# A first stage's instruction list made anew: maxima subtracted on VectorE for four sub-blocks, low parts of x formed in PSUM for five

## The chip, the cores and the metric

The kernel runs on one core of a Trainium2 chip. The metric is the device time of one execution in microseconds, as a median over runs; the traces show one execution each. TensorE is called PE in the views, VectorE DVE, ScalarE ACT, GpSimd POOL and SyncE SP. PE's weight loads stand apart as PEld.

## What is computed

```python
def _attn_ref(q, k, v):                      # batch 8, heads 8, seq 576, head_dim 64
    scores = scale * np.matmul(q_c, k_c.transpose(0, 1, 2, 4, 3))   # chunks of 64 tokens
    scores = scores - np.max(scores, axis=-1, keepdims=True)
    attn = np.exp(scores)
    attn = attn / (np.sum(attn, axis=-1, keepdims=True) + 1e-09)
    return np.matmul(attn, v_c)

def _moe_ref(x, w_in, w_out, alpha):         # x: 4608 tokens x 512, d_ff 2048
    h = x @ w_in
    g = np.maximum(h, 0.0) + alpha * np.minimum(h, 0.0)
    return g @ w_out
```

q, k and v are float32, the weights arrive as float64 patterns. The output of the attention, with the heads side by side, is x.

## The kernel before

The 4608 tokens make 36 sub-blocks of 128 tokens (two chunks of 64 each), and nine blocks of 512 tokens. The d_ff axis is cut into 16 slices f of 128. Every product of the two layers is made in three passes out of high and low parts (high x high, high x low, low x high), each of the matmuls 128x128 by 128x512. `h` of a block and a slice is 12 such matmuls into one bank of `ps_h` (line 422); its share of the output, called `o` here, is 12 more into `ps_oa` and `ps_ob` (line 458). Between the two, ACT forms the negative part (line 407), DVE the PReLU (410), ACT the high part `gh` (436) and DVE the low part `gl` (439). `ps_h` has two buffers, so an `h` can start only when line 410 of the `h` two before it has read its bank.

Blocks 0 and 1 (eight sub-blocks, the **first stage**) need their attention before anything else can run. Each sub-block s goes through scores `S` (line 261), maxima `m` (298), exponentials `z`/`e` (304 or 313), sums and normalisation `a`, `r`, `n` (317 to 323), four transposes `T` through PSUM (349), their copy `p` (356), values `V` (367), and the two parts of x: `x` (high, ACT, line 373) and `l` (low, DVE, line 375). The exponentials have two forms. A sub-block in `SUBTRACTED` has its maxima subtracted by DVE, one exponential over 128x512 on ACT, and its sums formed by DVE. The others have the maximum as ACT's bias, and so take eight exponentials of 128x64, each with its sum.

While that runs, weights are fetched (`wi3`, `wo3`: a DMA of 512 KB on SP's queue) and split: `wi3b`, `k`, `h`, `u`, `v`, `i`, `j` are the seven steps of `piece`, two on ACT and five on DVE (`wi0` has all on DVE).

All of this is an order written out by hand, the string `START`: each token makes its instructions, and every engine runs its own in the order of the list. `W8` are eight filler matmuls of 128x128 on zeros. `q`, `k`, `v` load two sub-blocks at a time. `h02 R02 G02 gh02 gl02 o02` are the steps of block 0, slice 2. `K0` to `K3` store the partial sums of block 0. `BANKS` names the PSUM banks that S, T and V of a sub-block use, `HALVES` the work buffer of a weight. The list ends with block 1, slice 7. After it a scheduler with a cost model of its own orders the instructions of the remaining steps; there the weights are fetched and split by `prepare`, and `keep_a` (line 597, POOL's queue) stores quarters of the split weights, from the moment at which POOL's `table` copy has seen the last part of x of block 1. Later stages, from block 2 on, are untouched.

Of the kernel before, what the change touches and what calls it, by code (L numbers as in the profile page):

```python
# [19 lines left out]
def bits(pattern):  # L20
# [5 lines left out]


START = """
W8 q0 k0 k1 q1 q2 S0 W1 k2 m0 S1 W5 wi1 z0 m1 e0 wi0 z1 a0 e1 r0 S2 k4 n0 S3 m2 q4 wi1b z2 T0 W6 m3
e2 a1 z3 wi1k v0 wi0b r1 wi1h n1 wi2 p0 wi0k T1 a2 e3 wi0h r2 S4 W3 v2 wi0u n2 m4 q6 p1 V0 a3 z4  # L30
wi0v e4 T2 W4 k6 r3 wi0i wi1u wi0j wo4 wi1v x0 V1 n3 p2 wo0 l0 x1 V2 wi2b a4 l1 T3 x2 wo1 wi2k S5 p3
l2 wi1i V3 m5 v6 S6 r4 x3 z5 n4 e5 wi4 l3 h00 m6 v4 wi2h z6 wi1j e6 wi2u S7 wi3 a5 wi2v h01 m7 wo2
r5 R00 z7 n5 wo0b G00 wi5 wi2i T5 e7 wo0k wi2j h02 wi7 a6 wo0h r6 wo0u wo5 n6 p5 wo0v gh00 T6 wo1b
a7 T4 wo3 gl00 wo0i V5 r7 wo1k p6 wo0j x5 V6 n7 p4 l5 x6 T7 wo1h V4 l6 p7 wo1u x4 o00 R01 wo1v wo2b
G01 wo1i l4 gh01 wo1j R02 V7 gl01 o01 x7 wo2k G02 wi4b wi3b wo2h wo2u gh02 l7 h10 wo2v gl02 wo2i
wi3k wo2j wi4k wo4b o02 wi3h wi4h R10 wo4k wi4u K0 wi3u K1 G10 h11 wi4v gh10 wi3v wi4i gl10 K2 wi3i
wo4h wi4j K3 o10 wo4u wo5b wi3j R11 wo4v wi5b G11 wo4i wo6 h12 wo5k gh11 wo4j wi6 gl11 wo3b wo5h
wo3k wo5u wo8 o11 R12 wo3h wo5v wi8 G12 wo5i wo3u gh12 wo7 h13 wo5j gl12 wi7b wo3v wi5k wo3i wi7k
wi5h o12 R13 wo3j wi5u G13 wi5v gh13 h14 wi7h wi5i gl13 wi6b wi5j wi6k wi7u wi6h o13 R14 wi7v G14
wi7i wi6u gh14 wo6b wi6v h15 gl14 wi6i wo6k wi6j wi7j wo7b wo6h o14 wo7k R15 wo6u G15 wo6v gh15 wo7h  # L40
wi8b gl15 h16 wo6i wo7u wo7v wo6j wo7i wi8k o15 wo7j R16 wo8b G16 wi8h gh16 wi8u gl16 h17 wi8v wo8k
wi8i wi8j wo8h o16 R17 G17 wo8u gh17 wo8v gl17 wo8i wo8j
"""
# [12 lines left out]
LISTED = 18

# [2 lines left out]
def tile_local_attention_prelu_ffn(  # L60
# [63 lines left out]
    def place(name, shape, dtype):  # L124
        return sides[name[:2]][0].tile(shape, dtype, name=name)
# [15 lines left out]
    FREE = 12  # L141
    RAWS = 6
# [89 lines left out]
    def attn_load(s, parts="qkv"):  # L232
# [61 lines left out]
    def early_softmax(s, sc3):  # L294
# [412 lines left out]
    banks = ["ps_h", "ps_h", "ps_o0", "ps_o1", "ps_o2", "ps_o3"]  # L707
# [171 lines left out]
    def start(token):  # L879

        name, at = re.fullmatch(r"([a-zA-Z]+)(\d+)([a-z]?)", token).group(1, 2)
        s = int(at)
        if name in ("wi", "wo"):
            if token[-1].isdigit():
                fetch(name, s)
            elif token[-1] == "b":
                running[name, s] = piece(name, s, f"{name}{s}" in ALONE)
                next(running[name, s])
            else:
                next(running[name, s])  # L890
# [190 lines left out]
```

## Time and profile before

| | us |
|---|---|
| median of 3 runs | 771.2 |
| lowest, highest | 770.76, 772.01 |
| span of the profiled execution | 770.2 |
| busy in the span: PE, DVE, ACT, POOL | 760.4, 646.7, 447.3, 184.8 |

The profiled execution is timed from its first to its last instruction; the median lies 1.0 us above its span, and no time of its own is listed beside the runs. PE's matmuls are pipelined and their ends are modelled, so start-to-start distances say more than durations; the last of a row's instructions reaches past the start of the next row. In a timeline a row is: start, duration, engine, line, operation, out<-in, shape, count, and in brackets the idle time of the engine before it and what ended it.

### The profile page before, as it was taken

Reading aid. Unit: us, or ns where it says so; the run is one execution under the profiler, and the core shown is the slowest. Engines: PE = TensorE matmul, PEld = TensorE weight load, DVE = VectorE, ACT = ScalarE, POOL = GpSimd, SP = SyncE. Lnnn points to the kernel's source line nnn. Section 1 sums busy time; section 2 is a strip of 40 time slices with the busy share of each in tenths; the row PEclk is TensorE's granted clock in tenths of the full one; section 3 lists DMA queues with packets and bytes.
Section 4 is the critical chain, followed back from the end, with each engine's and each line's share of the span. In section 5 each row is a group of like instructions: output and inputs, shape, how many; then the busy total and the mean of one; then the engine's idle time right before and its main releaser. Section 6 shows DMA issues by size and latency. Waiting matters only on the chain.

```text
span 770.2 us, 15415 instructions
## 1 busy us (share of the span) xinstructions
PE 760.4 (99%) x5558; PEld 639.8 (83%) x5558; DVE 646.7 (84%) x1140; ACT 447.3 (58%) x1221; POOL 184.8 (24%) x304
## 2 busy tenths in 40 slices
PE   7999999999999999999999999999999999999998
PEld 7788887888888888888888888888888888888886
DVE  6999988989899886877899898777898977679784
ACT  6975555576666665666657456664574544354643
POOL 1153322343254331111121121111221121122110
PEclk9999999999999999999999999999999999999999
DMA  9859496468798775878765678875656765555573
GB/s 349 337 196 386 176 324 216 163 229 226 234 238 274 240 258 200 304 275 277 263 234 197 233 250 288 269 239 206 207 193 223 260 228 193 204 205 192 198 258 144
DMA packets 69322, 184.52 MB, mean 240 GB/s; under 512 B 10992, under 2 KB 18176, under 8 KB 69120
## 3 DMA queue, kind: packets, MB, share of 16 engines
q0 software_dynamic: 34336, 119.56, 45.9%
q1 hardware_dynamic: 34480, 63.20, 24.2%
q8 instruction: 44, 0.72, 0.4%
q10 hardware_dynamic: 432, 0.79, 0.3%
q14 instruction: 30, 0.25, 0.1%
HBM read 135.27 MB, written 42.99 MB: 231 GB/s over the span
## 4 chain that ended last, share of the span: by engine, by line
PE 92%; ACT 4%; DVE 2%; DMA 2%; issue 0%; ACTq 0%; SPq 0%
PE ps_o L722 20%; PE ps_o L850 19%; PE ps_h L422 14%; PE ps_h L722 10%; PE ps_h L850 10%; PE ps_oa L458 8%; PE ps_ob L458 7%; PE ps_a L388 2%; PE ps_a L272 2%; ACT wi L313 1%; ACT wo L313 1%; DMA raw<-w_in 1%; DMA raw<-w_out 1%; PE ps_h L898 1%; ACT wi L207 0%
## 5 line engine op out<-in xcount | busy, mean ns | idle before, releaser
L422 PE MATMUL ps_h<-xh,wi 128*128 128x512 f32 x384 | 101.7, 385 | 0.7 <-DVE g L410 0.5
L422 PEld LDWEIGHTS ps_h<-xh,wi 128*128 128x128 f32 x384 | 70.7, 187 | 13.8 <-DVE g L410 0.9
L722 PE MATMUL ps_o<-wi,raw 128*128 128x512 f32 x336 | 79.1, 382 | 0.0
L722 PEld LDWEIGHTS ps_o<-wi,raw 128*128 128x128 f32 x336 | 62.5, 187 | 11.2
L678 ACT CAST gh<-wo 128x512 fp32r<-128x512 f32 x66 | 41.0, 620 | 47.4 <-PE ps_o L850 31.8
L287 ACT ACTIVATE pr<-ps_a,mx 128x64 f32<-128x64 f32 x224 | 67.2, 325 | 0.8
L458 PE MATMUL ps_oa<-wo,gh 128*128 128x512 f32 x192 | 58.5, 385 | 0.1
L458 PE MATMUL ps_ob<-wo,gh 128*128 128x512 f32 x192 | 57.7, 380 | 0.0
L422 PE MATMUL ps_h<-xl,wi 128*128 128x512 f32 x192 | 50.6, 381 | 0.0
L679 DVE TENSOR_TENSOR gl<-wo,gh 128x512 fp32r<-128x512 f32 x63 | 43.2, 686 | 7.5 <-ACT gh L678 7.1
L287 ACT ACTIVATION_READ_ACCUMULATOR pr<-ps_a,mx 128x1 f32 x224 | 48.6, 217 | 0.0
L659 POOL DMA_DIRECT2D raw<-wi_a x42 | 22.3, 531 | 102.1 <-PE ps_o L722 54.5
L659 POOL DMA_DIRECT2D raw<-wo_a x42 | 22.2, 529 | 90.8 <-PE ps_o L850 51.2
L407 ACT ACTIVATE wo<-gh 128x512 f32<-128x512 f32 x24 | 15.2, 632 | 48.5 <-DVE gh L752 48.5
L678 ACT CAST ta<-wo 128x512 fp32r<-128x512 f32 x42 | 26.1, 621 | 26.4 <-PE ps_o L850 15.2
L422 PEld LDWEIGHTS ps_h<-xl,wi 128*128 128x128 f32 x192 | 35.8, 187 | 6.7 <-DVE xl L375 0.2
L458 PEld LDWEIGHTS ps_ob<-wo,gh 128*128 128x128 f32 x192 | 35.9, 187 | 6.4
L458 PEld LDWEIGHTS ps_oa<-wo,gh 128*128 128x128 f32 x192 | 35.3, 187 | 7.0 <-ACT gh L436 0.5
L722 PE MATMUL ps_o<-wi,wo 128*128 128x512 f32 x168 | 40.4, 383 | 0.0
L722 PE MATMUL ps_o<-wi,wi 128*128 128x512 f32 x168 | 40.4, 383 | 0.0
L722 PE MATMUL ps_h<-wi,raw 128*128 128x512 f32 x168 | 40.4, 382 | 0.0
L407 ACT ACTIVATE g<-ps_h 128x512 f32<-128x512 f32 x48 | 29.5, 614 | 17.5 <-PE ps_h L422 17.5
(296 smaller groups left out, 2036.2 us busy)
## 6 DMA issues: line engine op xcount, KB each, us to landing
raw<-wi_a POOLq DMA_DIRECT2D x42, 512.0 KB, 4.4
raw<-wo_a POOLq DMA_DIRECT2D x42, 512.0 KB, 3.5
wi<-wi_a POOLq DMA_DIRECT2D x21, 512.0 KB, 3.7
wo<-wi_a POOLq DMA_DIRECT2D x21, 512.0 KB, 4.3
wi<-wo_a POOLq DMA_DIRECT2D x21, 512.0 KB, 3.5
wo<-wo_a POOLq DMA_DIRECT2D x21, 512.0 KB, 3.6
k_sb<-kT SPq DMA_DIRECT2D x28, 256.0 KB, 4.7
q_sb<-qT SPq DMA_DIRECT2D x28, 256.0 KB, 4.1
```

Of the source, the lines that this page charges most:

```text
L272: pe(nc.tensor.matmul(att[0][c * C:(c + 1) * C, par, (NP + hp) * C:(NP + hp + 1) * C], lhsT=q_sb[rows, 2 * hp + c], rhs=kb[rows, 2 * hp + ...
L287: last = nc.scalar.activation(pr[:, g], sc3[:, g // NP, g % NP], AF.Exp, bias=mx[:, g], scale=SCALE, accum_out=sm[:, g])
L313: last = nc.scalar.activation(pr[:, g], sc3[:, g % 2, g // 2], AF.Exp, bias=mx[:, g], scale=SCALE, accum_out=sm[:, g])
L388: pe(nc.tensor.matmul(att[0][par * C:(par + 1) * C, c, hp * C:(hp + 1) * C], lhsT=v_sb[rows, h * C:(h + 1) * C], rhs=p[rows, :, par * NP + ...
L407: nc.scalar.activation(g, h, AF.Relu, scale=-1.0)
L422: pe(nc.tensor.matmul(woven(hps), lhsT=wi[f][:, l, k * P:(k + 1) * P], rhs=woven(xx[:, k]), start=(i == 0 and k == 0), stop=(i == 2 and k ...
L458: pe(nc.tensor.matmul(woven(o), lhsT=a[:, ts], rhs=woven(wo[f][:, l]), start=(f == first and i == 0), stop=(f == last and i == 2),))
L659: streamed[0] = nc.gpsimd.dma_start(out=f32(t), in_=units[side][n])
L678: hi = nc.scalar.copy(t_hi, t)
L679: return hi, nc.vector.tensor_tensor(t_lo, t, f32(t_hi), op=ALU.subtract)
L722: pe(nc.tensor.matmul(woven(ps), lhsT=w[:, l, k * P:(k + 1) * P], rhs=woven(xx[:, xl]), start=first and at == 0, stop=at == n - 1, skip_gr ...
L850: pe(nc.tensor.matmul(woven(ps[m]), lhsT=w[:, l, m * P:(m + 1) * P], rhs=woven(xx), start=i in (1, 5, 2) and j == 0 and n == 0, stop=j == ...
```

## The change

The string `START` is replaced by another list, with `BANKS` and `HALVES` to match. Three things in it are done in another way. `SUBTRACTED` grows from sub-block 0 to 0, 2, 5 and 6. For the sub-blocks in `REMAINDERS` (0 to 4) the low part of x is no longer DVE's subtraction: after ACT has copied the high part, a new token `X` multiplies it by a negated identity on PE and accumulates onto the values in PSUM, and `l` is then an ACT copy of what is left. And a transpose takes a single bank, which can be one of `ps_h`, where it took a pair.

```diff
-W8 q0 k0 k1 q1 q2 S0 W1 k2 m0 S1 W5 wi1 z0 m1 e0 wi0 z1 a0 e1 r0 S2 k4 n0 S3 m2 q4 wi1b z2 T0 W6 m3
...
+k0 q0 W16 S0 m0 k1 q1 z0 W1 S1 e0 q2 m1 k2 z1 a0 r0 e1 W6 S2
...
-SUBTRACTED = (0,)
+SUBTRACTED = (0, 2, 5, 6,)
+REMAINDERS = (0, 1, 2, 3, 4,)
...
+    minus = room(FREE + RAWS + 1, [P, P], F32R)
+    nc.scalar.mul(minus, ident, -1.0)
...
+    pairs = {}
+
     def banks_of(token):
-        pool, name = ((ps_a, "ps_a"), (ps_o, "ps_oa"), (ps_o, "ps_ob"))[BANKS[token]]
-        return pool.tile([P, 2, TB], F32, name=name)
+        pair, bank = divmod(BANKS[token], 2)
+        if pair == 3:
+            return ps_h.tile([P, TB], F32, name="ps_h")
+        if pair not in pairs:
+            pool, name = ((ps_a, "ps_a"), (ps_o, "ps_oa"), (ps_o, "ps_ob"))[pair]
+            pairs[pair] = pool.tile([P, 2, TB], F32, name=name)
+        return pairs[pair][:, bank] if token[0] == "T" else pairs[pair]
...
             pe(nc.tensor.matmul(
-                xo[to, c, cols], lhsT=v_sb[rows, h * C:(h + 1) * C], rhs=p[rows, h * C:(h + 1) * C], start=True, stop=True,
+                xo[to, c, cols], lhsT=v_sb[rows, h * C:(h + 1) * C], rhs=p[rows, h * C:(h + 1) * C],
+                start=hp == 0 or s not in REMAINDERS, stop=True, skip_group_check=hp > 0,
             ))
...
-        nc.vector.tensor_tensor(xl, xo, f32(xh), op=ALU.subtract)
+        if s in REMAINDERS:
+            for c in range(2):
+                pe(nc.tensor.matmul(banks[:, c, :NP * C], lhsT=minus, rhs=xh[:, c], start=False, stop=True, skip_group_check=True))
+            yield
+            nc.scalar.copy(xl, xo)
+        else:
+            nc.vector.tensor_tensor(xl, xo, f32(xh), op=ALU.subtract)
```

Lines move down by 10 to 17 with it: 261 becomes 271, 313 becomes 323, 407 becomes 424, 410 becomes 427, 422 becomes 439.

The beginning of PE's list: fillers (into `ps_h`) and the scores of the first sub-blocks. Before:

```order
L898 MATMUL ps_h<-wo_109 128x128 x8
L261 MATMUL ps_oa<-wo_96,wo_98 64x64 x16
L898 MATMUL ps_h<-wo_109 128x128
L261 MATMUL ps_ob<-wo_96,wo_98 64x64 x16
L898 MATMUL ps_h<-wo_109 128x128 x5
```

And now:

```order
L915 MATMUL ps_h<-wo_109 128x128 x16
L271 MATMUL ps_ob<-wo_96,wo_98 64x64 x16
L915 MATMUL ps_h<-wo_109 128x128
L271 MATMUL ps_oa<-wo_96,wo_98 64x64 x16
L915 MATMUL ps_h<-wo_109 128x128 x6
```

Sixteen fillers stand where eight stood, ahead of the scores of sub-block 0.

ACT's list from the exponentials of sub-block 4 (into `wo_100`) to the last part of x that block 0 needs. Before:

```order
L313 ACTIVATE wo_100,sm<-ps_ob,mx 128x64 x8
L373 CAST xh<-ps_oa 128x2x4x64
L356 COPY wi_103<-ps_a 128x512
L373 CAST xh<-ps_ob 128x2x4x64
L194 ACTIVATE tc<-more 128x512
L373 CAST xh<-ps_a 128x2x4x64
L356 COPY wi_103<-ps_oa 128x512
L207 CAST wi_307<-ta 128x512
L373 CAST xh<-ps_oa 128x2x4x64
```

And now:

```order
L323 ACTIVATE wo_100,sm<-ps_a,mx 128x64 x8
L384 CAST xh<-ps_ob 128x2x4x64
L366 COPY wi_103<-ps_h 128x512
L384 CAST xh<-ps_oa 128x2x4x64
L390 CAST xl<-ps_ob 128x2x4x64
L366 COPY wi_103<-ps_h 128x512
L390 CAST xl<-ps_oa 128x2x4x64
L197 ACTIVATE tb<-raw 128x512
L384 CAST xh<-ps_ob 128x2x4x64
L384 CAST xh<-ps_a 128x2x4x64
L314 ACTIVATE wo_100<-wo_100 128x512
L390 CAST xl<-ps_ob 128x2x4x64
```

Four copies of low parts have come into it (the fourth is the next row, `xl<-ps_a`), and the exponential of sub-block 5 is one instruction.

PE's list just after the hand-written part ends, where block 1 meets slice 8 (`wi8`, split as `wi8_1152` before and `wi8_1160` now). Before, slices 7 and 8 of block 1 follow each other in `ps_h_1614` and `ps_h_1649`:

```order
L422 MATMUL ps_h_1614<-xh_122,wi7_1032 128x4x32x4 x4
L422 MATMUL ps_h_1649<-xh_122,wi8_1152 128x4x32x4 x4
L422 MATMUL ps_h_1649<-xl_123,wi8_1152 128x4x32x4 x2
L458 MATMUL ps_oa_1505<-wo6_1104,gh_1595 128x4x32x4 x2
L458 MATMUL ps_ob_1506<-wo6_1104,gh_1595 128x4x32x4 x2
```

Now, with `ps_h_1348` (slice 8 of block 1), `ps_h_1405` (slice 3 of block 0) and `ps_h_1478` (slice 4 of block 0):

```order
L439 MATMUL ps_h_1348<-xh_126,wi8_1160 128x4x32x4 x4
L439 MATMUL ps_h_1348<-xl_127,wi8_1160 128x4x32x4 x4
L439 MATMUL ps_h_1405<-xh_124,wi3_863 128x4x32x4 x4
L439 MATMUL ps_h_1405<-xl_125,wi3_863 128x4x32x4 x4
L439 MATMUL ps_h_1405<-xh_124,wi3_863 128x4x32x4 x4
...
L475 MATMUL ps_ob_973<-wo7_1133,gl_1231 128x4x32x4
L439 MATMUL ps_h_1348<-xh_126,wi8_1160 128x4x32x4 x4
L439 MATMUL ps_h_1478<-xh_124,wi4_880 128x4x32x4 x4
```

The third pass of slice 8 has moved behind a whole `h` and a whole `o`, directly ahead of the next `h`, which takes the same bank of `ps_h`.

## Rows read from the trace of the kernel before

**Rows 1.** The page's head: the span.

```profile
span 770.2 us, 15415 instructions
```

**Rows 2.** Two stretches: length, busy time of each engine, clock granted, DMA share, GB/s.

```profile
0.00:45.00 45.00, 39.44 (x663) 33.15 (x664) 37.63 (x81) 36.34 (x149) 5.97 (x17) 1.00 0.75 294
45.00:120.00 75.00, 75.00 (x343) 63.74 (x342) 70.59 (x132) 44.21 (x75) 28.64 (x39) 1.00 0.83 296
```

**Rows 3.** Chain of waits of the first 50 us: start, us, what.

```profile
14.48 2.32 ACT wi L313 x16
...
17.05 2.66 ACT wo L313 x16
```

**Rows 4.** Timeline of PE, first stage.

```profile
1.06 3.78 PE L898 MATMUL ps_h<-wo 128*128 128x128 f32 x16 [1.06 <-DVE table L147]
4.77 1.13 PE L261 MATMUL ps_oa<-wo,wo 64*64 64x64 f32 x32
...
6.56 0.97 PE L261 MATMUL ps_ob<-wo,wo 64*64 64x64 f32 x32
...
11.64 1.50 PE L898 MATMUL ps_h<-wo 128*128 128x128 f32 x12
...
15.06 0.69 PE L261 MATMUL ps_ob<-wo,wo 64*64 64x64 f32 x32 [0.34 <-DMA wo<-qT]
...
27.73 1.15 PE L422 MATMUL ps_h<-xh,wi 128*128 128x512 f32 x4
...
30.49 0.60 PE L349 MATMUL ps_ob<-ident,wo 128*128 128x128 f32 x4
...
33.57 0.60 PE L349 MATMUL ps_oa<-ident,wi 128*128 128x128 f32 x4
...
37.80 0.72 PE L458 MATMUL ps_oa<-wo,gh 128*128 128x512 f32 x2
...
44.06 1.04 PE L422 MATMUL ps_h<-xh,wi 128*128 128x512 f32 x4
```

**Rows 5.** Timeline of DVE, first stage.

```profile
5.97 0.69 DVE L298 TENSOR_REDUCE mx<-ps_oa 128x8 f32<-128x512 f32 x1 [4.96 <-PE ps_oa L261]
...
12.70 0.37 DVE L198 TENSOR_SCALAR ta<-ta 128x512 uint32<-128x512 uint32 x1
...
15.23 0.68 DVE L323 TENSOR_TENSOR wi<-wi,sm 128x512 f32<-128x512 f32 x1
15.84 0.68 DVE L298 TENSOR_REDUCE mx<-ps_ob 128x8 f32<-128x512 f32 x1
16.56 0.17 DVE L309 TENSOR_SCALAR mx<-mx 128x8 f32<-128x8 f32 x1
```

**Rows 6.** Timeline of ACT, first stage.

```profile
21.00 0.73 ACT L194 ACTIVATE tc<-more 128x512 f32<-128x512 f32 x1
21.58 0.62 ACT L373 CAST xh<-ps_a 128x512 fp32r<-128x512 f32 x1
22.05 0.64 ACT L356 COPY wi<-ps_oa 128x512 f32<-128x512 f32 x1
```

**Rows 7.** Timelines of PE, ACT and DVE around the end of an h.

```profile
93.34 1.92 PE L422 MATMUL ps_h<-xh,wi 128*128 128x512 f32 x8
...
94.42 0.60 ACT L407 ACTIVATE g<-ps_h 128x512 f32<-128x512 f32 x1 [1.38 <-PE ps_h L422]
...
95.05 0.75 DVE L410 SCALAR_TENSOR_TENSOR g<-g,rise,ps_h 128x512 f32<-128x512 f32 x1
```

**Rows 8.** PE's waits from 40 us on; then a wait of ACT (timeline).

```profile
PE ps_h L422 <- DVE g L410: 0.5, 1, 0.5
...
120.58 0.70 ACT L194 ACTIVATE tc<-raw 128x512 f32<-128x512 f32 x1 [2.35 <-DMA raw<-w_out]
```

**Rows 9.** Timelines of SP's queue and of POOL.

```profile
48.83 0.33 SPq L495 DMA_DIRECT2D partial<-wo  x1
...
44.25 0.58 POOL L953 COPY table<-xl 128x1 f32<-128x1 f32 x1 [10.78 <-DVE xl L375]
```

More of the change, by code (lines that the diff above doesn't have):

```diff
@@ L28 @@
 START = """
-W8 q0 k0 k1 q1 q2 S0 W1 k2 m0 S1 W5 wi1 z0 m1 e0 wi0 z1 a0 e1 r0 S2 k4 n0 S3 m2 q4 wi1b z2 T0 W6 m3
[L30 to L39, printed above, removed]
@@ L40 @@
-wi7i wi6u gh14 wo6b wi6v h15 gl14 wi6i wo6k wi6j wi7j wo7b wo6h o14 wo7k R15 wo6u G15 wo6v gh15 wo7h
-wi8b gl15 h16 wo6i wo7u wo7v wo6j wo7i wi8k o15 wo7j R16 wo8b G16 wi8h gh16 wi8u gl16 h17 wi8v wo8k
-wi8i wi8j wo8h o16 R17 G17 wo8u gh17 wo8v gl17 wo8i wo8j
+k0 q0 W16 S0 m0 k1 q1 z0 W1 S1 e0 q2 m1 k2 z1 a0 r0 e1 W6 S2
+n0 wi0 m2 S3 m3 z2 wi0b a1 q4 W3 T0 p0 k4 r1 z3 v0 wi0k k6 e2 n1
+W9 S4 wi0h e3 a2 T1 m4 q6 r2 p1 z4 S5 a3 n2 m5 e4 v2 r3 W3 V0
+x0 z5 wi0u T2 W4 V1 S6 X0 a4 n3 T3 p2 x1 wi0v l0 m6 r4 p3 z6 wi1
@@ new lines @@
+X1 V2 wi0i V3 l1 wi1b x2 x3 n4 S7 wi0j wi1k m7 T4 wi1h X2 z7 wi2 v4 e5
+l2 wi1u X3 a5 l3 wi1v h00 p4 wi2b r5 V4 wi2k wo0 n5 e6 wi1i e7 wo2 a6 wo0b
+a7 wi2h v6 x4 T5 p5 R00 r6 wi1j h01 X4 wo1 n6 r7 wi2u T6 l4 wi7 wi4 n7
+wo0k wi2v wo0h T7 p6 V5 p7 G00 wo0u wi2i V6 wi2j V7 R01 x7 G01 x6 wo3 wo2b x5
+gh00 wo1b l7 l6 l5 h02 wo0v h10 gl00 gh01 wo0i wo0j R02 wo1k G02 wi3 o00 gh02 wo1h wo2k
+wo1u h11 wo2h wo1v wo2u gl01 wo1i wo1j wo4 o01 wi7b wi3b wo2v wo2i gl02 wo8 wi7k wo2j wi3k R11
+R10 G11 wi4b wi3h gh11 o02 wi5 wi7h G10 wi3u wi3v K2 gl11 wo5 h12 gh10 wi3i wi7u wi4k wi3j
@@ new lines @@
+K3 wi5b h13 wi4h K0 K1 gl10 wi5k wi4u R13 wi5h wi4v wi5u wi7v R12 wi7i o10 o11 wi4i wi5v
+G12 wi5i wi4j wi7j wo7 wi5j wo3b gh12 wi6 wo3k gl12 wo3h wi6b G13 wo3u wi8 wi6k h14 wo4b wo6
+wo3v gh13 wi6h gl13 wi6u wo3i wo3j h15 wo4k wi6v wo5b wo5k o12 o13 wi6i R14 wo5h wo4h wi6j wo4u
+G14 h16 wo5u wo6b gh14 wo4v wo4i wo6k gl14 R15 wo6h wo4j wo7b wo5v wo6u G15 wo6v wo5i wo5j gh15
+gl15 wo6i wo6j o14 wi8b wo7k R16 G16 wo7h gh16 wi8k wo7u wo8b wi8h wo8k gl16 h17 o15 R17 wo8h
+wo8u wi8u wi8v wi8i wo7v wo8v G17 wo7i wo7j wo8i wo8j gh17 o16 gl17 wi8j
@@ L43 @@
 """
 ALONE = ('wi0',)
-SUBTRACTED = (0,)
+SUBTRACTED = (0, 2, 5, 6,)
+REMAINDERS = (0, 1, 2, 3, 4,)
 HALVES = {
-    "wi1": "ta", "wi0": "tb", "wi2": "tc", "wo0": "tb", "wo1": "ta", "wo2": "tc", "wi4": "tb", "wi3": "ta",
-    "wo4": "tc", "wo5": "tb", "wi5": "ta", "wo3": "tc", "wi7": "tb", "wi6": "tc", "wo6": "ta", "wo7": "tc",
-    "wi8": "tb", "wo8": "ta",
+    "wi0": "ta", "wi1": "tb", "wi2": "tc", "wi3": "tc", "wi4": "tb", "wi5": "tc", "wi6": "ta", "wi7": "ta", "wi8": "tb", "wo0": "ta", "wo1": "tc", "wo2": "tb", "wo3": "tb", "wo4": "tc", "wo5": "tb", "wo6": "ta", "wo7": "tc", "wo8": "ta",
@@ L51 @@
 }
 BANKS = {
-    "S0": 1, "S1": 2, "S2": 0, "S3": 1, "T0": 2, "T1": 0, "S4": 2, "V0": 1, "T2": 0, "V1": 2, "V2": 0, "T3": 1,
-    "S5": 2, "V3": 1, "S6": 0, "S7": 1, "T5": 2, "T6": 1, "T4": 2, "V5": 0, "V6": 1, "T7": 2, "V4": 0, "V7": 0,
+    "S0": 4, "S1": 2, "S2": 0, "S3": 4, "S4": 0, "S5": 2, "S6": 0, "S7": 2, "T0": 2, "T1": 7, "T2": 7, "T3": 6, "T4": 7, "T5": 0, "T6": 1, "T7": 0, "V0": 4, "V1": 2, "V2": 4, "V3": 0, "V4": 4, "V5": 2, "V6": 4, "V7": 0,
 }
@@ L346, in early_transpose @@
         pr = probs.pop(s)
-        tp = banks_of(f"T{s}")[:, 0]
+        tp = banks_of(f"T{s}")
         for hp in range(NP):
@@ L367, in early_values @@
             pe(nc.tensor.matmul(
-                xo[to, c, cols], lhsT=v_sb[rows, h * C:(h + 1) * C], rhs=p[rows, h * C:(h + 1) * C], start=True, stop=True,
+                xo[to, c, cols], lhsT=v_sb[rows, h * C:(h + 1) * C], rhs=p[rows, h * C:(h + 1) * C],
+                start=hp == 0 or s not in REMAINDERS, stop=True, skip_group_check=hp > 0,
             ))
         yield
-        xo = by_chunk(xo)
+        banks, xo = xo, by_chunk(xo)
         xh, xl = (tokens(t, s) for t in x[s // SPB])
@@ L910, in start @@
             next(running["values", s])
-        elif name in ("x", "l"):
+        elif name in ("x", "X", "l"):
             next(running["values", s])
```

## The prediction

> **What bounds the kernel now.** I read the busy time by stretches first. From 45 to 120 us PE has 75.00 us of work in 75, and of the first 45 us it is busy 39.44 [rows 2]. In a span of 770.2 us [rows 1] this is a kernel in which PE never rests once the first stage is over, so the change can act in three ways only: by the moment at which PE is through the first stage's work, by PE work that comes in or goes, and by waits of PE behind it. In the first stage itself ACT has 36.34 us of work and DVE 37.63 in 45 [rows 2]; neither has much room. The chain of waits, read next, goes there through ACT's exponentials: 2.32 us for the eight of a sub-block at 14.48, 2.66 from 17.05, each with its read of the sum, so that they count x16 [rows 3]. Third come the timelines of PE, DVE and ACT, which give the distance from one start to the next.
>
> As a fixed mark I take 44.06, where PE starts the fourth `h` of block 0 [rows 4]. By then it has done all scores, transposes and values, and five units, three `h` and two `o` (a unit is 12 matmuls of 128x512). In the new list the same work is done at the end of `o00`, after `h00`, `h01`, `h02`, `h10`. How much later or earlier PE gets there is what the first stage gives, since all PE work behind it is as before.
>
> **The start of the list.** A filler takes two passes: 16 rows for `W8`, which run from 1.06 until the scores start at 4.77, 0.23 us each; later 12 of them take 1.50, 0.125 each [rows 4]. So PE has two paces, 1.8 to 1, and the scores show when it changes: 32 passes last 1.13 at 4.77, 0.97 at 6.56 and 0.69 at 15.06 [rows 4]. The group at 6.56 is thus (0.97 - 0.69) / (1.13 - 0.69) = 0.64 at the slow pace, and the change falls near 7.2. The row on the granted clock has 1.00 over the first 45 us [rows 2] and doesn't resolve it. `W16` is 32 passes: 26 at 0.23 reach 7.1, six at 0.125 end at 7.8, and S0 starts there instead of 4.77, some 3 us later. If the pace rises already with the 17th pass, it is 6.8 (+2.0); if it never rises in the fillers, 8.5 (+3.7).
>
> The Trainium skill ("TensorE: Matmul & The Clock Gate", section "What's actually happening") says that the array starts at 1.2 GHz and goes to 2.4 GHz after it has been kept busy, at a moment that differs from run to run. The two paces agree with the two levels; by this rule the closed row of fillers could raise the clock no later than the broken one of before, which is the first rival below.
>
> **DVE up to the exponentials of sub-block 4.** From scores to their maximum it is 0.78 (15.06 [rows 4] to 15.84 [rows 5]), so DVE's first maximum comes at 8.5, where it came at 5.97 [rows 5]. DVE was free there for 4.96 us before, so nothing absorbs the delay. From this maximum to the normalisation after which ACT can start sub-block 4, the new list has 12 instructions of full size at 0.61 (15.23 to 15.84) = 7.3, three of the integer or scalar kind at 0.3 (0.37 long at 12.70) = 0.9, eight small ones at 0.1 (0.17 long) = 0.8, and seven places where an instruction wants its neighbour's result, 0.12 each (15.84 to 16.56 is 0.72, not 0.60) = 0.9 [rows 5]. Together 9.9, so these exponentials start at 18.4 to 18.5 instead of 17.05 [rows 3]: 1.4 us of the 3 remain, since two of the sums and some steps of `piece` stand later than before. This is where subtracting maxima on DVE costs: three more subtractions and three more sums.
>
> **ACT from there.** ACT now has a closed stretch until the low parts that `h00` needs for its second pass. Eight exponentials 2.33 (bound 2.66 [rows 3]); six casts and copies at 0.47 (21.58 to 22.05) = 2.8; one magnitude at 0.58 (21.00 to 21.58); two casts 0.94; one whole exponential 0.58, by the magnitude, which has its size; one low part 0.47; the last to its end 0.62 [rows 6]. Sum 8.3, so the second pass of `h00` starts at 26.8. Two of these low parts were DVE's before, which is the cost; one exponential instead of eight saves 2.33 - 0.58 = 1.75 for each of three sub-blocks, against 5 x 0.47 = 2.4 for five low parts, a net gain of 2.9 for ACT. Of that only what lies ahead of 26.8 acts on the mark.
>
> **PE from there to the mark.** The rest of `h00` is 8 of 12 matmuls, 2.76 x 8/12 = 1.84 (27.73 to 30.49 is 2.76 for twelve); `h01` 2.76; seven transposes and values at 0.70 (33.57 to 37.80 is 4.23 for six, with their waits) = 4.9 [rows 4]; `h02`, `h10`, `o00` at 2.64 = 7.9: four matmuls in a row last 1.04 (44.06) [rows 4], eight 1.92 (93.34) [rows 7], so one more is 0.88 / 4 = 0.22 and twelve are 2.64. New work is one pair of `X` (two matmuls of 128x256): by half of 0.22 each it is 0.2, and by a matmul of four passes of a transpose's kind at most 0.9; I take 0.2, as their operand is of the type of the `h` matmuls. The other four pairs fall in the stretch that ACT sets and cost nothing as long as it does; uncovered they cost four times as much as the one. Sum 26.8 + 17.6 = 44.4 to 44.5 against 44.06: **+0.4**, bounds -0.8 (early pace, and pieces at 0.6) and +1.1 (slow pace, `X` dear).
>
> **Behind the list.** The third pass of slice 8 now stands directly ahead of an `h` that takes the same bank. That `h` can't start until ACT and DVE have read the bank. At the end of an `h` of before this reads: the row at 93.34 is eight matmuls, four that end an `h` and four that begin the next, which could start at 93.34 + 4 x 0.22 = 94.22; ACT takes the first `h` up at 94.42, DVE at 95.05 and is done at 95.80 [rows 7]. Where the next `h` has to wait for that, PE stands 95.80 - 94.22 = **+1.6**. Before, the `h` behind it had the other bank, and there is no wait of PE at that place: from 40 us on its only wait is 0.5 us, for DVE's line 410 [rows 8]. Bounds: 1.4, and 2.2 if DVE is in the middle of a full-size instruction. Nothing behind it on PE could fill in, since PE works in order.
>
> **Later weights.** ACT waits 2.35 us for a weight at 120.58 [rows 8], so loads are near the edge there. The loads stand on SP's queue behind the stores of partial sums, the first at 48.83, and these follow PE's outputs, which come some 2 us later by the terms above; POOL's stores, which wait for the last part of x (44.25), can start earlier, as that part's sub-blocks come some 5 us earlier in the new list [rows 9]. Both want the same transfers. The 0.5 us of before may go (-0.5), or one or two such waits come in up to +2; I take +0.2.
>
> At nothing: `minus`, a small ACT instruction while ACT waits for the first maximum (if that cover went, 0.1); the shorter sums on POOL, whose results nobody waits for in the chain; transposes in single banks, which change buffers and not work.
>
> **Sum**: +0.4 + 1.6 + 0.2 = +2.2. On the profiled execution the span goes from 770.2 [rows 1] to 772.4; the median of before lies 1.0 us above its span, so the median comes to **773.4 us**. About 0.2 %, 1.5 us, is what can be told from no change here: faster is below 769.7, slower above 772.7.
>
> **Rivals.** (1) The pace rises with the first fillers, S0 starts at 6.8, and all up to the mark comes 1.0 to 1.4 us earlier: -0.8 + 1.6 + 0.2 = +1.0, 772.2, no difference. For it: the fillers are a closed row now. Against: 16 of them ended at the slow pace in before. Chance 0.22. (2) Faster: ACT, not DVE, sets the first stage in both kernels, and its net gain of 2.9 is paid in full at the mark; with the wait of 0.5 gone and the stall of 1.6 it is -1.8, 769.4. It decides if `o00` ends before 41.3. For it: the chain runs over ACT's exponentials. Against: DVE's list to 18.5. Chance 0.17. (3) Weights late: partial stores and POOL's stores collide, PE waits up to 2 us more between 70 and 120: 775.4. For it: ACT's 2.35 us wait. Against: PE had only 0.5 us of waits. Chance 0.13. (4) That the list does not do what it says, because the scheduler behind it undoes it, is excluded by the order of the instructions. The forecast keeps 0.48.
>
> **How the numbers follow.** The forecast's own range by its bounds is 772.0 to 774.7, a quarter of it under 772.7. Faster: 0.17, rival 2. Same: 0.22 of rival 1 and 0.12 of the forecast, with 0.02 of rival 3: 0.36. Slower: the rest, 0.47. The range takes in rival 1 and most of rival 3 and reaches to the edge of rival 2: 769.6 to 775.8.
>
> **What would show it.** Right: S0 near 7.8, DVE's first maximum near 8.5, sub-block 4's exponentials near 18.5, `h00`'s second pass near 26.8, the end of `o00` near 44.5, and after the list one PE wait of 1.6 us for DVE's line 427 (the PReLU). Wrong at once: an `o00` that ends before 43 or after 46, or no such wait of PE; POOL's copy of `table` later than 44.25; a PE wait of over 1 us for a weight's low part past 70 us.

## The result, and the profile after

The changed kernel takes 779.79 us (median of 4, 779.17 to 782.96) against 771.13 before: a ratio of 1.0115, 95% interval [1.0094, 1.0136]. The forecast was 773.4, its range 769.6 to 775.8. The sign was right, the size wrong by a factor of nearly four. The profiled execution is 7.2 us longer than that of before [rows 1].

The head of its page and its row on the instruction queue (packets, MB, share); its two stretches that answer to [rows 2]; and PE's waits from 40 us on, which answer to [rows 8]:

```profile
span 777.4 us, 15471 instructions
...
PE 764.9 (98%) x5598; PEld 644.9 (83%) x5598; DVE 646.8 (83%) x1141; ACT 444.5 (57%) x1182; POOL 182.8 (24%) x301
...
q8 instruction: 45, 0.74, 0.4%
```

```profile
0.00:45.00 45.00, 39.36 (x684) 34.79 (x685) 31.53 (x70) 31.21 (x105) 5.69 (x17) 0.96 0.81 304
45.00:120.00 75.00, 73.22 (x332) 61.53 (x331) 71.90 (x135) 44.52 (x77) 24.88 (x33) 1.00 0.74 254
```

```profile
PE ps_h L439 <- DVE g L427: 1.5, 1, 1.5
PE ps_oa L475 <- ACT gh L453: 1.3, 1, 1.3
PE ps_h L439 <- ACT wi L210: 0.2, 1, 0.2
```

ACT and DVE have 31 us of work in the first 45, where they had 36 and 38, and yet less is done. PE's timeline says why (start, duration, engine, line, operation, shape, count, and in brackets the idle time before it):

```profile
1.06 5.33 PE L915 MATMUL ps_h<-wo 128*128 128x128 f32 x32 [1.06 <-DVE table L148]
6.31 0.69 PE L271 MATMUL ps_ob<-wo,wo 64*64 64x64 f32 x32
...
23.00 0.45 PE L271 MATMUL ps_oa<-wi,wi 64*64 64x64 f32 x17
27.49 0.46 PE L271 MATMUL ps_oa<-wi,wi 64*64 64x64 f32 x15 [4.04 <-issue]
...
29.49 1.91 PE L439 MATMUL ps_h<-xh,wi 128*128 128x512 f32 x4
...
48.23 1.04 PE L439 MATMUL ps_h<-xh,wi 128*128 128x512 f32 x4
```

PE stops for 4.04 us in the middle of the scores of sub-block 7, after 17 of 32 matmuls that read the same tiles, and what ends it is put down to "issue": no engine and no load that the profile shows. The mark of the prediction, the end of `o00`, is the row at 48.23; before, the same work was done at 44.06 [rows 4]. So 4.17 of the 7.2 us are lost in the first stage, 3.0 behind it.

The medians are 8.7 us apart and the spans 7.2, and this needs no cause in the kernel: a listed time is 1.7 to 1.9 us longer than its span in all executions, so the traced execution of before (770.2) is the longest of its runs, 772.01, and that of the changed kernel the shortest, 779.17.

The DMA queues in two stretches inside this wait (queue, kind: packets, MB, share of 16 engines), 23.2 to 25.2 and 25.2 to 26.2:

```profile
q1 hardware_dynamic: 227, 0.85, 103.4%
```

```profile
q1 hardware_dynamic: 108, 0.39, 96.0%
q8 instruction: 1, 0.02, 5.6%
```

The loads keep all 16 engines busy, and while PE stands, one packet of the kind `instruction` comes through. There are 45 of these in the execution, 0.74 MB, so 16.4 KB each; 2 x 5598 matmuls and weight loads by 45 are 249 a packet. With PE's semaphore and drain instructions, which the trace lists but does not count as busy, PE has 11,527 instructions, 256 a packet. The packet itself lies at 25.24 to 26.13 us, and PE goes on 1.4 us after its end.

### The profile page after: what moved, and what is told of

Read it like the earlier page. It is cut to its first block, busy times and chain, and to the rows that moved or that the text cites. A ratio compares the mean times of both kernels' runs of the same rounds, so it can differ in the third digit from the quotient of the medians.

```text
span 777.4 us, 15471 instructions
## 1 busy us (share of the span) xinstructions
PE 764.9 (98%) x5598; PEld 644.9 (83%) x5598; DVE 646.8 (83%) x1141; ACT 444.5 (57%) x1182; POOL 182.8 (24%) x301
## 4 chain that ended last, share of the span: by engine, by line
PE 88%; DVE 5%; DMA 4%; issue 1%; ACT 1%; SPq 0%; ACTq 0%
PE ps_o L739 19%; PE ps_o L867 19%; PE ps_h L439 12%; PE ps_h L739 10%; PE ps_h L867 10%; PE ps_oa L475 6%; PE ps_ob L475 6%; PE ps_a L405 2%; PE ps_a L282 2%; PE ps_h L915 2%; DMA raw<-w_in 1%; DMA raw<-w_out 1%; DMA wi<-w_in 1%; DVE gl L456 1%; DMA more<-w_in 1%
## 5 line engine op out<-in xcount | busy, mean ns | idle before, releaser
L695 ACT CAST gh<-wo 128x512 fp32r<-128x512 f32 x66 | 41.0, 621 | 47.1 <-PE ps_o L867 31.5
L696 DVE TENSOR_TENSOR gl<-wo,gh 128x512 fp32r<-128x512 f32 x63 | 43.2, 686 | 7.5 <-ACT gh L695 7.1
L453 ACT CAST gh<-g 128x512 fp32r<-128x512 f32 x48 | 30.0, 627 | 16.9 <-DVE g L427 10.8
```

The costliest lines, as they stand in the source:

```text
L453: nc.scalar.copy(gh, g)
L695: hi = nc.scalar.copy(t_hi, t)
L696: return hi, nc.vector.tensor_tensor(t_lo, t, f32(t_hi), op=ALU.subtract)
```

## Experiments

The theory, F: PE had used up its instructions, and the next 16 KB stood behind the loads on the DMA engines. The rivals: D, the scores wait for a part of q or k; C, PE is held back after dense work.

**e1_wide.** Same columns of fillers, fewer instructions:

```diff
-            for _ in range(s):
-                nc.tensor.matmul(hps[:, :P], lhsT=plain, rhs=plain, start=True, stop=True)
+            for width in [TB] * (s // 4) + [P] * (s % 4):
+                nc.tensor.matmul(hps[:, :width], lhsT=plain[:, :P], rhs=plain[:, :width], start=True, stop=True)
```

> The changed kernel, with PE's fillers given as matmuls of 128x512 wherever four of 128x128 stand in a row: the same columns, so the same busy time, out of 18 instead of 42 matmuls, which is 96 fewer of PE's records (a filler has four) ahead of the scores of sub-block 7. Theory F (instruction fetch): PE stood 4.0 us in the middle of these scores because it had used up its instructions and the next 16 KB of them came late, behind the loads on the same DMA engines. Then the wait shrinks to 1 us or less, o00 ends at 43.5 to 44.5 instead of 48.2, and the time is 773.5 to 775.5. Rival D (data: the scores wait for a part of q or k that the views don't show): the wait of 4 us stays at the same matmul, 779 to 780. Rival C (PE is held back after a stretch of dense work, as with its clock): the stretch is as dense, the wait stays, 779 to 780.

It took 778.17 us, ratio 1.0097 [1.0077, 1.0117]: 1.6 less than the changed kernel, which these runs hardly tell from nothing, and not the 4 to 6 expected. The wait in sub-block 7's scores is gone (they run from 24.2 to 24.8), but three others put down to issue are there, in the values of other sub-blocks; the mark is at 46.08:

```profile
23.26 0.63 PE L377 MATMUL ps_ob<-wi,wi 64*64 64x64 f32 x27 [0.28 <-issue]
...
29.64 0.56 PE L377 MATMUL ps_ob<-wo,wo 64*64 64x64 f32 x19 [0.33 <-issue]
...
37.63 0.46 PE L377 MATMUL ps_a<-wi,wi 64*64 64x64 f32 x15 [1.36 <-issue]
```

That they move with the number of instructions, and not with the work, is seen when PE's records up to a wait are counted. The next rows give stretches from 0 to the moment of a wait; the numbers in brackets behind PE and PEld are the matmuls and weight loads done. The changed kernel at the beginning and the end of its wait:

```profile
0.00:23.30 23.30, 21.80 (x473) 19.96 (x474) 15.29 (x37) 14.79 (x62) 2.54 (x11) 1.00 0.91 338
0.00:27.40 27.40, 21.96 (x473) 20.04 (x474) 16.23 (x38) 16.45 (x65) 2.54 (x11) 1.00 0.93 349
```

And e1_wide at its three:

```profile
0.00:23.20 23.20, 21.06 (x346) 13.58 (x346) 14.91 (x35) 13.84 (x61) 2.54 (x11) 1.00 0.88 319
0.00:29.60 29.60, 27.08 (x473) 18.34 (x473) 21.07 (x49) 20.16 (x77) 2.54 (x11) 1.00 0.91 340
0.00:37.60 37.60, 33.60 (x599) 24.01 (x600) 28.35 (x64) 26.60 (x96) 2.89 (x12) 1.00 0.93 350
```

PE stands at 692, 946 and 1199 records, 254 and 253 apart, and the second is the place at which the changed kernel stood with other work in hand (946 and 947 records). With the semaphore instructions counted too, the three places lie behind 705, 961 and 1217 instructions, 256 apart, and the changed kernel stood behind its 961st. The packets end at 21.57, 28.12 and 36.17, each 1.5 to 1.7 us before PE goes on. Neither D nor C gives that.

**e2_dense.** The other direction, on the kernel before:

```diff
-            for _ in range(s):
-                nc.tensor.matmul(hps[:, :P], lhsT=plain, rhs=plain, start=True, stop=True)
+            few = s in (3, 4, 6)
+            n = P // 2 if few else P
+            for _ in range(5 * s if few else s):
+                nc.tensor.matmul(hps[:n, :n], lhsT=plain[:n, :n], rhs=plain[:n, :n], start=True, stop=True)
```

> The kernel before, with 13 of its 27 fillers (those in rows of 6, 3 and 4) given as five times as many of 64x64, about as long in PE's time: 208 more PE records ahead of sub-block 7's scores, nothing else changed. Theory F: PE runs out of instructions here too, a wait put down to issue of 1 to 4 us between 18 and 30 us, and the time is 772 to 776. Rivals D and C: no such wait, 770.5 to 772.

778.56 us, 1.0099 [1.0085, 1.0113]: the old list becomes slower by 7.6 us, but not by records alone. The smaller fillers were to take about as long, and they take longer. The fillers of the first 30 us, before and here (length, PE's busy time, PEld's, clock, DMA share, GB/s):

```profile
0.00:30.00 30.00, 9.46 (x54) 8.31 (x54) 1.00 0.95 372
```

```profile
0.00:30.00 30.00, 13.84 (x158) 12.83 (x158) 0.97 0.96 378
```

PE's waits for issue in it, and its records up to the second:

```profile
20.96 1.03 PE L900 MATMUL ps_h<-wo 64*64 64x64 f32 x15 [0.64 <-issue]
...
27.11 0.51 PE L367 MATMUL ps_oa<-wi,wi 64*64 64x64 f32 x19 [1.90 <-issue]
```

```profile
0.00:27.05 27.05, 21.55 (x473) 19.40 (x474) 17.48 (x41) 17.02 (x77) 3.15 (x12) 1.00 0.95 373
```

Again 947 records, in a kernel with another list; the first wait comes behind 693. F stands on these places, not on the price. The mark, at 49.64, is 5.6 us later than before: 2.0 are there already where the values before the second wait begin (24.77 against 22.74), by the longer fillers and the first wait, 1.9 are the second wait, and `h00` behind it takes 1.5 longer, as the granted clock is low there, as in the changed kernel:

```profile
27.50:31.50 4.00, 3.78 (x50) 2.98 (x40) 3.12 (x7) 3.78 (x24) 0.53 (x1) 0.61 1.04 422
```

**e3_gate.** PE's list as in the changed kernel, the traffic thinned. A token `Z0` makes a small load wait for ACT, and holds the loads behind it on SP's queue:

```diff
-x0 z5 wi0u T2 W4 V1 S6 X0 a4 n3 T3 p2 x1 wi0v l0 m6 r4 p3 z6 wi1
+x0 z5 wi0u T2 W4 V1 S6 X0 a4 n3 T3 p2 x1 wi0v l0 m6 r4 wi1 p3 Z0 z6
+        elif name == "Z":
+            nc.scalar.copy(rest[:, :1], table)
+            nc.sync.dma_start(out=rest[:, :1], in_=alpha[:, :1])
```

> The changed kernel, PE's list untouched; the loads from the third weight on stand behind a small load that waits for ACT's copy of the transposes of sub-block 3 (21.8 us), so that the DMA engines run dry at about 21 to 22 us. Theory F with the fetch delayed by the traffic of the loads: PE's wait of 4.0 us shrinks to 1 us or less, though weights come 3 to 5 us later and may cost elsewhere; 774 to 779. F without the traffic (a fetch takes 5 us anyhow): the wait stays at 3.5 to 4. Rival D: it stays at 4 or grows.

776.23 us, 1.0069 [1.0054, 1.0083]. A stretch of it (the last two numbers: DMA share, GB/s), the one with 947 records, and PE's rows:

```profile
20.00:25.00 5.00, 5.00 (x150) 4.34 (x143) 4.66 (x12) 5.00 (x12) 0.36 (x1) 1.00 0.27 44
```

```profile
25.85 1.17 PE L439 MATMUL ps_h<-xl,wi 128*128 128x512 f32 x4
...
29.46 0.69 PE L377 MATMUL ps_ob<-wo,wo 64*64 64x64 f32 x32 [1.55 <-DMA wo<-v]
...
44.40 1.04 PE L439 MATMUL ps_h<-xh,wi 128*128 128x512 f32 x4
```

With DMA at 0.27 instead of full, PE works through the whole stretch, 5.00 of 5.00 us, with the same instructions in the same order. The packet comes 4.4 us earlier, at 20.81 to 21.76, where the stretch from 20.8 to 21.8 holds no load:

```profile
q8 instruction: 1, 0.02, 5.9%
```

So in the changed kernel the packet is late because of the loads. It is just in time here: PE passes the place at 23.08, 1.3 us after its end. The mark is at 44.40, though PE now waits 1.55 for values that were held back.

**e12_w8.** One part of the change undone:

```diff
-k0 q0 W16 S0 m0 k1 q1 z0 W1 S1 e0 q2 m1 k2 z1 a0 r0 e1 W6 S2
+k0 q0 W8 S0 m0 k1 q1 z0 W1 S1 e0 q2 m1 k2 z1 a0 r0 e1 W6 S2
```

> The changed kernel with W8 in the place of W16, one part of the change undone: 32 of PE's 961 records less ahead of the wait, the scores 0.7 to 1.5 us earlier. Theory F: the packet that PE waits for is asked for by records, not by time, and PE still stands at its 961st record, now a little further on in the work; the wait is 3 to 4 us, the end of o00 at 46.5 to 48, the time 777.5 to 779.5. If the long row of fillers itself was the fault, the wait is gone: 774 to 776.

778.25 us, 1.0088 [1.0072, 1.0104]; the mark at 46.90. The long row of fillers is not the fault:

```profile
21.75 0.57 PE L271 MATMUL ps_a<-wi,wi 64*64 64x64 f32 x21 [1.26 <-issue]
...
28.01 0.49 PE L359 MATMUL ps_h<-ident,wo 128*128 128x128 f32 x3 [2.59 <-issue]
```

```profile
0.00:27.95 27.95, 21.68 (x473) 19.30 (x474) 18.55 (x43) 16.52 (x65) 2.35 (x11) 1.00 0.94 357
```

With 32 records less, PE stands at the same 947th, now in sub-block 4's transposes behind these scores (the expectation's 961 counts semaphore instructions too). The waits are in part spread: 0.82 at 15.68 and 1.26 at 21.75 come behind 441 and 694 records, again 253 apart.

**e4_tail.** The waits behind the list:

```diff
-wo8u wi8u wi8v wi8i wo7v wo8v G17 wo7i wo7j wo8i wo8j gh17 o16 gl17 wi8j
+wo8u wi8u wi8v wi8i wi8j wo7v wo8v G17 wo7i wo7j wo8i wo8j gh17 o16 gl17
```

> The changed kernel with one token moved: the last step of weight slice 8 (wi8j) stands eight places earlier on DVE, and the scheduler then puts the third pass of block 1, slice 8, right behind its first two. The wait of 1.5 us for line 427 at 99 to 101 us goes, nothing else in the first 50 us changes: 778.0 to 778.6 instead of 779.8, if no other wait comes in its place. Rival: the weights are late at that place (ACT waits for loads nearby), PE waits for them instead, 779 to 780.

779.45 us, 1.0106 [1.0093, 1.0119], no difference to the changed kernel that these runs can tell. The rival in the expectation named the wrong engine, but the gain does return as another wait: PE waits from 40 us on are

```profile
PE ps_h L439 <- DVE g L427: 1.2, 3, 0.5
PE ps_h L439 <- ACT wi L210: 0.2, 1, 0.2
```

One wait of 1.5 has become three of 0.4; the wait of 1.3 for ACT at 139 us did go. From the mark to the end of the span this kernel needs 777.4 - 49.15 = 728.3 us, the changed one 777.4 - 48.23 = 729.2, that of before 770.2 - 44.06 = 726.1.

**e5_gate2** opens the gate earlier, behind `p2`, with `v4` first behind it; **e6_gate_tail** is e5_gate2 with the token of e4_tail moved too.

```diff
-x0 z5 wi0u T2 W4 V1 S6 X0 a4 n3 T3 p2 x1 wi0v l0 m6 r4 p3 z6 wi1
+x0 z5 wi0u T2 W4 V1 S6 X0 a4 n3 T3 wi1 p2 Z0 v4 x1 wi0v l0 m6 r4 p3 z6
```

> As e3_gate, with the small load behind ACT's copy of the transposes of sub-block 2 instead of 3 and the values of sub-blocks 4 and 5 first behind it, so that PE does not wait 1.6 us for them. Theory F: no wait in sub-block 7's scores and none for these values, the end of o00 at 42.6 to 43.8 (44.4 in e3_gate, 48.2 in the changed kernel, 44.06 before); the first stage itself is then a gain of about 1, and what stays on the other side comes after 80 us (1.5 and 1.3 us of PE's waits): 773.5 to 775.5. Rival: the loads only change places, another wait of 1 us or more comes into the first stage, o00 at 44.4 or later, 776.

> e5_gate2 with the token wi8j moved as in e4_tail. In e4_tail the wait of 1.5 us gave way to three of 0.4 on the mean. If those came only from the loads that were late there after PE's long wait, they are gone here, and the time is 1.3 to 1.6 below e5_gate2; if they belong to the list's end as such (DVE is full there), it is 0.2 to 0.5 below.

777.07 us (1.0084 [1.005, 1.0118]) and 780.84 (1.0094 [1.0064, 1.0124]): both missed. PE waits for issue again, behind 947 records, in e5_gate2 1.44 us and in e6_gate_tail 2.9, the mark being at 45.14 and 47.38; the packet ends at 24.29 and 26.55. That the loads come back too early is not shown to be the reason: in e5_gate2 they all but stop from 21 to 22 (second row below), and the packet begins at 23.12 all the same. What it waited for there stays open. The comparison of the two says nothing about the list's end, as this wait differs between them by as much as what was to be measured.

```profile
25.66 0.46 PE L271 MATMUL ps_oa<-wi,wi 64*64 64x64 f32 x15 [1.44 <-issue]
...
21.00:22.00 1.00, 1.00 (x40) 0.93 (x36) 0.28 (x1) 0.83 (x3) 0.00 (x0) 1.00 0.01 4
```

**e7_two** and **e8_noremainder** take a part of the change out of e5_gate2: `SUBTRACTED = (0, 5, 6,)`, and `REMAINDERS = ()` with no `X` in the list.

> e5_gate2 with sub-block 2 taken out of SUBTRACTED: DVE has one subtraction and one sum less (1.2 us), ACT eight exponentials instead of one (1.7 us more). If DVE sets the pace up to sub-block 4's exponentials, as the prediction has it, they start no later, and o00 ends within 0.5 us of e5_gate2. If ACT sets it, they start 1.2 to 1.7 later and o00 ends 1 to 1.7 later.

> e5_gate2 with REMAINDERS empty and no X in the list: ten matmuls of 128x256 less on PE, five copies of 0.47 less on ACT, five subtractions of 0.61 more on DVE. If the low parts on ACT are what holds h00 back, as the prediction's ACT sum has it, its second pass starts 0.5 to 1 earlier; if DVE is the engine with no room, it starts 0.5 to 2 later and o00 ends later by as much.

```diff
-SUBTRACTED = (0, 2, 5, 6,)
+SUBTRACTED = (0, 5, 6,)
```

```diff
-REMAINDERS = (0, 1, 2, 3, 4,)
+REMAINDERS = ()
```

e7_two: 779.16, 1.0093 [1.0073, 1.0113]. Sub-block 4's exponentials start at 19.37 (17.81 in e5_gate2); the first scores are 0.6 later too, so 1.0 of it is the edit: nearer to the answer "ACT sets it". The end of `o00` cannot be read, for PE waits 2.4 for issue there. e8_noremainder: 781.55, 1.0122 [1.0104, 1.0141]. The second pass of `h00` starts 2.3 later than in e5_gate2 (28.12), 0.5 of it by the later scores:

```profile
30.45 2.08 PE L439 MATMUL ps_h<-xl,wi 128*128 128x512 f32 x4 [2.29 <-DVE xl L392]
```

PE waits for DVE's low part. Forming low parts on PE and ACT is thus worth having in this list: DVE has no room for five more subtractions.

**e9_all**, **e10_all_w8**, **e13_w8_wide_tail**, **e14_w8_wide_tail_gate** put edits together (wide fillers, `wi8j` earlier; `W8` in the last three; a gate behind `p3` in the first two, none in e13, one behind `p2` with both weights ahead in e14). **e11_before_wide** is the kernel before with the edit of e1_wide. What is new in the lists, of e9 and e10, and of e14:

```diff
-x0 z5 wi0u T2 W4 V1 S6 X0 a4 n3 T3 p2 x1 wi0v l0 m6 r4 p3 z6 wi1
+x0 z5 wi0u T2 W4 V1 S6 X0 a4 n3 T3 p2 x1 wi0v l0 m6 r4 wi1 p3 Z0 v4 z6
```

```diff
-x0 z5 wi0u T2 W4 V1 S6 X0 a4 n3 T3 p2 x1 wi0v l0 m6 r4 p3 z6 wi1
+x0 z5 wi0u T2 W4 V1 S6 X0 a4 n3 T3 wi1 wi2 p2 Z0 v4 x1 wi0v l0 m6 r4 p3 z6
```

> The changed kernel with all three edits: fillers as matmuls of 128x512 (e1_wide), the loads from v of sub-blocks 4 and 5 on behind a small load that waits for ACT's copy of the transposes of sub-block 3 (e3_gate, but these values first), wi8j earlier (e4_tail). Theory: the change loses by PE's wait for instructions and by the waits at the end of its list, and its first stage is otherwise level with before or up to 1 us shorter. Then PE has no wait over 0.5 us put down to issue between 15 and 45 us, o00 ends at 43.0 to 44.5, and the time is 771 to 773 (before: 771.1). If the first stage itself is what is longer, o00 ends at 45 or later and the time is 774 or more.

> e9_all with W8 in the place of W16 at the start. The prediction has 16 fillers delay the first scores. If their start sets the first stage, scores begin 0.5 to 1.5 us earlier than in e9_all and o00 ends as much earlier. If the closed row of fillers is what brings PE's clock up early, and the stage is set by DVE and ACT behind it, o00 stays within 0.5 us.

> The kernel before with its fillers given as 128x512 wherever four stand in a row: 60 of PE's records less, the same columns. Theory F says that PE had its instructions only 1 to 3 us ahead of their use in the kernel before, so that fetching did not hold it up: 770.5 to 772, no difference. If its row of PE waits put down to issue was already such a wait, it gains 0.5 to 1.5 us.

> The changed kernel with W8, fillers of 128x512 and wi8j earlier, the loads as they were: 128 fewer PE records ahead of the wait. Theory F: no single wait of 2 us put down to issue, but some of 0.5 to 1.5 at 16 KB boundaries, as in e1_wide; o00 at 44 to 46, 773.5 to 775.5.

> e13_w8_wide_tail with the loads behind the second weight of the first layer held until ACT's copy of the transposes of sub-block 2, so that neither PE waits for instructions nor ACT for that weight (2.5 us in e9_all, 1.8 in e10_all_w8). If the new first stage is shorter once its waits for instructions are gone, o00 ends at 42.5 to 43.5 and the time is 772 to 773.5, since about 2 us of waits stay behind the list; if it is not, o00 ends at 44 or later, 774 or more.

| | median us | ratio to before, 95% | end of o00 | PE's longest waits, 12 to 45 us |
|---|---|---|---|---|
| e9_all | 777.57 | 1.0071 [1.0058, 1.0084] | 48.88 | 2.0 DVE, 1.6 issue |
| e10_all_w8 | 774.43 | 1.0043 [1.0031, 1.0055] | 44.30 | 1.4 DVE |
| e13 | 774.99 | 1.0045 [1.003, 1.0061] | 44.62 | 1.1 issue, 0.6 DVE |
| e14 | 775.68 | 1.0057 [1.0038, 1.0076] | 46.84 | 2.7 issue |
| e11_before_wide | 772.14 | 1.0013 [1.0004, 1.0021] | 43.83 | 1.0 DVE, 0.9 DMA |

e9_all and e14 came out on the slower side of their expectations, e10_all_w8 on neither, e13 as expected, and e11 just above its range. In e9_all the gate makes a weight late, first row, and PE still runs out later, second row:

```profile
29.31 0.66 ACT L197 ACTIVATE tc<-more 128x512 f32<-128x512 f32 x1 [2.49 <-DMA more<-w_in]
...
40.45 0.46 PE L377 MATMUL ps_a<-wi,wi 64*64 64x64 f32 x15 [1.56 <-issue]
```

e10_all_w8 is the best version of the new list, 5 us better than the changed kernel and still 3.1 behind the old one. Its `o00` ends 4.6 us earlier than in e9_all, far more than its scores' earlier start (5.17 against 6.88), as PE has no wait for issue over 0.2 us in it; the question of its expectation, whether the scores' start sets the stage, is not answered by that. e14 shows the other side: 2.7 us at the boundary of 599 + 600 records. Its executions lie between 771.92 and 778.59, a spread that the kernel before (770.53 to 773.33 beside it) has not. e11 gives no sign that the old list was held up by its instructions: with fewer of them it is 0.8 us slower, not faster. Why is not shown: PE starts 0.4 us later, as a zero tile four times as large is needed first, but its first scores start at 4.78 against 4.77, and `o00` ends earlier.

## Why the prediction was wrong, point by point

**The missing term.** The part on PE from the start of the list to the mark counts durations of PE's work and waits for other engines; it has no term for the supply of instructions. This is the step that failed: 4.04 us in the profiled execution, for a cost put at nothing without a reason. PE's work in the new list is denser where the loads are thickest. The old list did 947 records by 29.16 us:

```profile
0.00:29.16 29.16, 24.20 (x473) 20.67 (x474) 22.28 (x52) 22.38 (x112) 4.28 (x14) 1.00 0.95 371
```

The changed kernel was there at 23.3, 5.9 us earlier, and the packet came at 25.2 to 26.2. For the some 254 records ahead of this place, from a packet's boundary to the next, the old list takes 6.8 us and the new one 3.3, both with DMA full:

```profile
22.40:29.16 6.76, 6.52 (x131) 5.22 (x128) 6.72 (x16) 6.46 (x37) 1.02 (x2) 1.00 1.02 416
```

```profile
20.00:23.30 3.30, 3.30 (x127) 3.02 (x126) 2.65 (x7) 3.21 (x7) 0.36 (x1) 1.00 1.03 420
```

Counted from the beginning of these stretches, the next packet is through after 4.5 us in the old list (26.91) and after 6.1 in the new one (26.13); in e3_gate, from the same boundary, it is 2.0 (19.76 to 21.76). The Trainium skill ("Runtime: NRT & Kernel Launch", section "Instruction fetch mechanics") says that an engine's instructions are refilled in blocks of 16 KiB, 256 instructions, over a DMA queue of its own while it works on the block before, and that the cost is mostly hidden. The size agrees (16.4 KB, 256 instructions a packet with the semaphores, 253 or 254 records between two waits); that it is hidden holds for the kernel before and not for this one. That page was not weighed in the prediction; it would have pointed to the question.

**What the wait brings with it.** Behind it the granted clock falls. 27.5 to 31.5 us of the changed kernel (the third number from the end is the clock):

```profile
27.50:31.50 4.00, 4.00 (x28) 3.55 (x28) 3.25 (x9) 2.20 (x5) 0.00 (x0) 0.57 1.02 419
```

0.57 on the mean is for most of the time the lower level, 1.2 GHz. `h00` takes 33.30 - 29.49 = 3.8 us there instead of 2.76. So about 1 us comes on top. Without wait and slow stretch the mark would be near 48.23 - 4.04 - 1.0 = 43.2, an estimate; 44.40 was measured in e3_gate and 44.30 in e10_all_w8, each with a wait of 1.4 to 1.55 that the gate brought in.

**The start.** S0 was to start at 7.8 and started at 6.31, below the range's 6.8. The clock rose within the first row of fillers: rival 1 held in this execution. It varies: with the same row of 16 fillers the scores started at 6.86 in e5_gate2 and at 7.45 in e7_two.

**DVE and ACT.** The lengths were right. DVE's first maximum comes 0.77 behind the scores' start (0.78), sub-block 4's exponentials 10.2 behind it (9.9):

```profile
7.08 0.69 DVE L308 TENSOR_REDUCE mx<-ps_ob 128x8 f32<-128x512 f32 x1 [6.07 <-PE ps_ob L271]
```

```profile
17.27 0.31 ACT L323 ACTIVATE wo<-ps_a,mx 128x64 f32<-128x64 f32 x1 [0.56 <-DVE wi L333]
```

ACT's stretch from there to `h00`'s second pass was to take 8.3; in e3_gate, where PE has no wait for instructions, it is 25.85 - 17.27 = 8.6. From there to the mark 17.6 were worked out; 44.40 - 25.85 - 1.55 = 17.0 were measured. The wait of ACT ahead of 17.27 is for DVE, as the prediction has it, but e7_two indicates that ACT is hardly less full: with seven exponentials more it is 1.0 later.

**Behind the list.** The wait for line 427 was worked out as 1.6 and is 1.55; the prediction has mechanism, place (99 to 101 us, not 95, as all is later) and size right:

```profile
100.63 1.15 PE L439 MATMUL ps_h<-xh,wi 128*128 128x512 f32 x4 [1.55 <-DVE g L427]
```

**Later weights**: +0.2 was taken, up to +2 allowed; it is about +1.1. The 0.5 of before went, and PE waits 1.34 at 139.2 for ACT's `gh` and 0.24 at 90.9. ACT stands behind a load, the mechanism named:

```profile
137.98 0.67 ACT L197 ACTIVATE tc<-raw 128x512 f32<-128x512 f32 x1 [2.75 <-DMA raw<-w_in]
```

**The sum anew.** 4.0 for instructions, 1.0 for the clock, 1.55 and 1.1 behind the list, less about 0.9 for the earlier start: 6.8 of the 7.2 us between the spans. The 0.4 that are left stay open; a longer execution of the changed kernel has a span of 781.1, but no trace that shows where. Without the first two the spans would differ by 2.2 us, the very sum of the forecast, and that is chance: by these figures the first stage comes out 1.3 better than worked out (-0.9 for +0.4), and what lies behind the list 1.2 dearer (3.0 for 1.8). Of the signs of being wrong one came, an `o00` that ends after 46.

**The rivals.** None was this one. Rival 2 (ACT's lighter load paid in full) wanted an `o00` that ends before 41.3; no kernel with the new list had one before 44.30, and the estimate above for PE fed is 43.2. About 1 us of it may be there, but no kernel had the stage free of other waits. No version beat the kernel before.

## What to carry to other kernels

Count an engine's instructions as well as its time: where small matmuls are packed densely while loads fill all DMA engines, ask whether 256 instructions go by faster than a 16 KB packet gets through (here 3.3 us against 6.1). A wait put down to issue in the middle of a row of like instructions, at the same count of records in different kernels, is the sign of it; the 0.4 us put down to issue ahead of sub-block 0's transposes, behind 361 records in the changed kernel and 300 in e1_wide, is not of this kind. Removing such a wait by holding loads back or by larger instructions moves the limit more readily than it lifts it, so compare the whole stage, not the one wait.

## What the runs showed of the hardware that was not expected

- Between the end of the instruction packet and PE's going on lie 1.4 us in the changed kernel (26.13 to 27.49), and 1.2 to 1.7 in the other kernels' waits at such a count, but for one of 0.7 in e8_noremainder.
- A wait of PE by 4.0 us was followed by half the clock; 2.4 in e7_two and 1.9 in e2_dense too, and, for DVE instead of instructions, 2.3 in e8_noremainder (granted 0.59 from 30.4 to 34.4 us); 2.9 in e6_gate_tail, 2.6 in e12_w8 and 1.4 in e5_gate2 were not. What decides between them is not told by these runs.
- A small matmul saves less than its size suggests: 60 passes of 64x64 fillers run from 10.99 to 14.72 in e2_dense, 0.062 us each, where a pass of 128x128 takes 0.125 [rows 4]. Five of them in the place of one are thus 2.5 times as long.
